# Attention and bilinear feed-forward on one core: the last tile's bias as two minima, low parts and q's split ordered behind the reciprocal, two subtractions of x ordered behind the gate product

## The chip, the cores and the metric

The kernel runs on one core of a Trainium2 chip. The metric is the device time of one execution in microseconds (us), the median over the runs shown. The kernel before took 1290.13 us (median of three runs, 1284.51 to 1292.95). The profile and the trace are those of one further execution. A core has five engines with a queue of instructions each: TensorE (PE in the profile, its weight loads are PEld), VectorE (DVE), ScalarE (ACT), GpSimd (POOL) and SyncE (SP), which here issues transfers. Each queue is worked off in order.

## The reference

Block-causal attention over 8 batches of 8 heads, 576 positions and 64 dimensions, then a bilinear feed-forward layer over all 4,608 tokens with 512 model and 1,536 inner dimensions, all in float32:

```python
def _attn_ref(q, k, v):
    B, H, S, D = q.shape                      # 8, 8, 576, 64
    block, scale = 64, 1.0 / np.sqrt(D)
    scores = scale * np.matmul(q, k.transpose(0, 1, 3, 2))
    pos = np.arange(S)
    mask = (pos[:, None] // block) >= (pos[None, :] // block)
    scores = np.where(mask, scores, -1000000000.0)
    scores = scores - np.max(scores, axis=-1, keepdims=True)
    attn = np.exp(scores)
    attn = attn / (np.sum(attn, axis=-1, keepdims=True) + 1e-09)
    return np.matmul(attn, v)

def reference(q, k, v, moe_w_a, moe_w_b, moe_w_out):
    o = _attn_ref(q, k, v)                    # 8, 8, 576, 64
    x = o.transpose(0, 2, 1, 3).reshape(4608, 512)
    return ((x @ moe_w_a) * (x @ moe_w_b)) @ moe_w_out
```

## The kernel before, in words

**Precision.** Most products are made from a high and a low part: a copy to the type fp32r on ACT (names with `h`: `ah`, `xh`, `hh`) and the rest, source minus copy, on DVE or POOL (names with `l`: `al`, `xl`). The first eight heads work in plain float32 (`NATIVE`).

**Attention, a head.** The queries of a head stand in tiles of 128 rows, t = 0 to 3, where tile t sees the keys up to its own end; the 64 rows at both ends of the sequence share one *side tile*. `softmax(i)` makes the scores of the side tile and of tile 3 on PE, then their negated maxima `nm` on DVE (line 400). These two tiles overlap: the rows in the lower half of the partitions have scores in both, so that both need the smaller of their two negated maxima, while in the upper half each tile keeps its own. The two columns of the bias `nb` (line 421) hold that. Exponentials run on ACT with `nm` or `nb` as bias and leave sums in `sm` (line 403). Tiles 0, 1 and 2 follow. Then DVE makes the row sums `rc` (lines 434 and 438) and their reciprocal (line 441), and POOL multiplies the exponentials `e` by it (line 444), tile by tile from 3 down.

`turn(i)` follows for t = 3 down to 0: PE transposes the scaled exponentials into `tp` (line 467), of which there are two buffers in PSUM, ACT copies it to `ah` (line 469), and DVE subtracts to give the low part `al` (line 471). A `tp` buffer is free for the tile after next when both have been done. `values(i)` multiplies v by `ah` (line 516) and by `al` (lines 520 and 522).

**Attention, the loop.** A slot handles one head: the table `SLOT` puts the maxima of head s, the transposes of heads s - 1 and s - 2 and the values of head s - 2 in turn. Heads go in pairs (even, odd), whose q and k are loaded together (lines 324 and 325, `kp` and `qp`), split into high and low (`split_q`, line 341; `split_k`, line 346) and spread by further transfers on SP (lines 360 and 361). In the even slot stand the split and the loads of a later pair.

**The first pass of the feed-forward layer** (`first_pass`, 4 of 12 tiles of the inner dimension) runs on PE in between: its products (line 217, `ps` from `xh` and `xl`, 128x288) fill PE between the steps of the heads. `convert_w` meanwhile turns the weights into the form that PE uses, from 512 KB loads `raww` (line 124). The last third of the kernel are two more passes (`ps_` = 0 and 1) over six pairs of token tiles of 384 tokens. `sums_x` loads and combines x (lines 664 to 688): differences on DVE (674 to 676 and 679, `xt`), high parts on ACT (677 to 681), low parts on DVE (684, 685) and, for the second half of the rows (`kp` = 1), on POOL (687, 688). `pair_unit` makes the products of one inner tile in PSUM banks `psy`, `psx`, `psw`, `psv` (line 705) and the gate product `u` on DVE (lines 723 to 733), from which ACT and POOL make the high and the low part of h (lines 110 and 113). `pair_out` multiplies by the output weights (line 751), adds the partial sum of the pass before on DVE (line 810) and stores it (line 811). Partial sums are loaded at line 806. The generator for the next tile's x is started in the fourth inner tile's turn and its remaining steps run ahead of `pair_out`. The *switch of passes* is the place, at about 1000 us in the trace, where pass 0's last tile ends and pass 1's first begins; the x of pass 1's first tile has the name `0_6`.

**What sets the order.** All this is written as one program; a scheduler then arranges the instructions of each engine by its own priorities. `behind_of(ins, key)` adds an order without a wait: `ins` shall stand behind the instruction that `last[key]` names. Keys are "nb" (the bias), "rc" (the row sums) and "hf" (the last gate product `u` of an inner tile). Before the change the sums stand behind "nb", as do the low parts of the tile that is transposed together with the side tile (`SIDE_T`) and of tile 0; the conversion of weights is paced by "hf".

## Time and profile before

| what | value |
|---|---|
| median of the runs (lowest, highest) | 1290.13 us (1284.51, 1292.95) |
| the profiled execution | 1293.99 us |
| its span in the trace | 1292.2 us |
| its mean granted clock of TensorE | 0.984 |
| instructions in the trace | 23401 |
| moved by transfers | 196.58 MB, mean 152 GB/s |

The span runs from the first to the last recorded instruction; the execution's own time has 1.8 us more around it. Stretches in the trace are counted from the span's start. Attention with the first pass fills it up to about 625 us, the end of the first pass and the turn to the second goes to 720, pass 0 to about 1000 and pass 1 to the end. Here is the granted clock in 40 equal slices of 32.3 us, in tenths (9 is 90% or more), beside the busy share of PE and VectorE:

```profile
PE   9998999999999999999998998999999899999998
DVE  6877778778878787887789999899976576577563
PEclk8999999999999999999998999999999899999999
```

And this is the chain that ended last, followed back from the last instruction, as shares of the span by engine and by line:

```profile
PE 61%; DVE 21%; issue 6%; DMA 5%; ACT 4%; POOL 2%; SPq 0%; ACTq 0%; DVEq 0%; POOLq 0%
PE pso_z L751 13%; PE ps L217 8%; PE psx_z L705 6%; PE psw_z L705 6%; PE psv_z L705 6%; PE tp L467 5%; DVE al L471 3%; PE s L394 3%; PE pso L217 3%; DVE nm L400 3%; PE psy_z L705 3%; PE av L522 2%; PE av L506 2%; POOL e L444 2%; DMA kp<-kT 1%
```

A row of a timeline reads: start in us, length, engine, line, operation, what it writes and reads with shapes, and in brackets how long the engine was idle before it and what ended that. A row of groups reads: line, engine, operation and operands, number, then busy time in us, mean in ns, idle time before.

### The profile page before, as it was taken

Reading aid. Unit: us, or ns where it says so; the run is one execution under the profiler, and the core shown is the slowest. Engines: PE = TensorE matmul, PEld = TensorE weight load, DVE = VectorE, ACT = ScalarE, POOL = GpSimd, SP = SyncE. Lnnn points to the kernel's source line nnn. Section 1 sums busy time; section 2 is a strip of 40 time slices with the busy share of each in tenths; the row PEclk is TensorE's granted clock in tenths of the full one; section 3 lists DMA queues with packets and bytes.
Section 4 is the critical chain, followed back from the end, with each engine's and each line's share of the span. In section 5 each row is a group of like instructions: output and inputs, shape, how many; then the busy total and the mean of one; then the engine's idle time right before and its main releaser. Section 6 shows DMA issues by size and latency. Waiting matters only on the chain.

```text
span 1292.2 us, 23401 instructions
## 1 busy us (share of the span) xinstructions
PE 1242.7 (96%) x7849; PEld 1177.4 (91%) x7849; DVE 1000.4 (77%) x2325; ACT 686.9 (53%) x1722; POOL 545.0 (42%) x681
## 2 busy tenths in 40 slices
PE   9998999999999999999998998999999899999998
PEld 5677989999999999999997998999999899999998
DVE  6877778778878787887789999899976576577563
ACT  5787777788787887887745423233322222222210
POOL 4667555555565555655522223223123123123231
PEclk8999999999999999999998999999999899999999
DMA  5466667766676666677224355464466442242131
GB/s 194 138 188 169 170 170 180 176 166 171 165 182 171 168 178 164 163 187 172 82 93 149 111 190 163 163 195 157 159 205 238 160 148 65 83 147 87 61 98 62
DMA packets 93496, 196.58 MB, mean 152 GB/s; under 512 B 11968, under 2 KB 52928, under 8 KB 93376
## 3 DMA queue, kind: packets, MB, share of 16 engines
q1 hardware_dynamic: 88768, 185.64, 50.8%
q10 hardware_dynamic: 4608, 9.44, 2.0%
q8 instruction: 63, 1.03, 0.3%
q14 instruction: 57, 0.47, 0.1%
HBM read 96.47 MB, written 47.19 MB: 111 GB/s over the span
## 4 chain that ended last, share of the span: by engine, by line
PE 61%; DVE 21%; issue 6%; DMA 5%; ACT 4%; POOL 2%; SPq 0%; ACTq 0%; DVEq 0%; POOLq 0%
PE pso_z L751 13%; PE ps L217 8%; PE psx_z L705 6%; PE psw_z L705 6%; PE psv_z L705 6%; PE tp L467 5%; DVE al L471 3%; PE s L394 3%; PE pso L217 3%; DVE nm L400 3%; PE psy_z L705 3%; PE av L522 2%; PE av L506 2%; POOL e L444 2%; DMA kp<-kT 1%
## 5 line engine op out<-in xcount | busy, mean ns | idle before, releaser
L113 POOL TENSOR_TENSOR h_z<-u_z,h_z 128x384 fp32r<-128x384 f32 x96 | 112.9, 1176 | 400.8 <-ACT h_z L110 378.2
L217 PE MATMUL ps<-xh,wab 128*128 128x288 f32 x1024 | 245.9, 306 | 0.0
L444 POOL TENSOR_SCALAR e<-e,rc 128x512 f32<-128x512 f32 (+3 forms) x256 | 152.3, 608 | 154.6 <-DVE rc L441 148.1
L751 PE MATMUL pso_z<-h_z,wo 128*128 128x384 f32 x1152 | 203.8, 335 | 3.5 <-POOL h_z L113 3.5
L751 PEld LDWEIGHTS pso_z<-h_z,wo 128*128 128x128 f32 x1152 | 199.6, 188 | 5.8 <-POOL h_z L113 5.8
L471 DVE TENSOR_TENSOR al<-tp,ah 128x512 fp32r<-128x512 f32 x224 | 138.8, 620 | 63.7 <-ACT ah L469 61.6
L217 PEld LDWEIGHTS ps<-xh,wab 128*128 128x128 f32 x1024 | 173.7, 190 | 3.6
L467 PE MATMUL tp<-ident,e 128*128 128x128 f32 x832 | 136.3, 279 | 18.5 <-POOL e L444 11.6
L217 PE MATMUL ps<-xl,wab 128*128 128x288 f32 x512 | 152.8, 299 | 0.2 <-POOL xl L113 0.2
L110 ACT CAST h_z<-u_z 128x384 fp32r<-128x384 f32 x96 | 49.4, 514 | 167.2 <-DVE u_z L730 162.1
L469 ACT CAST ah<-tp 128x512 fp32r<-128x512 f32 x224 | 119.2, 534 | 35.0 <-PE tp L467 33.3
L467 PEld LDWEIGHTS tp<-ident,e 128*128 128x128 f32 x832 | 99.3, 142 | 36.2 <-POOL e L444 21.4
L217 PE MATMUL pso<-hh,wo 128*128 128x288 f32 x512 | 128.5, 312 | 3.2 <-ACT hh L110 3.2
L705 PE MATMUL psx_z<-xh,wab 128*128 128x384 f32 x384 | 118.5, 344 | 9.0 <-DVE u_z L723 8.6
L403 ACT ACTIVATE e<-s,nm 128x192 f32<-128x192 f32 (+2 forms) x192 | 101.8, 531 | 36.7 <-DVE nm L400 30.1
L705 PE MATMUL psw_z<-xh,wab 128*128 128x384 f32 x384 | 117.3, 341 | 0.8 <-DVE u_z L725 0.8
L705 PE MATMUL psv_z<-xh,wab 128*128 128x384 f32 x384 | 117.2, 340 | 0.5 <-DVE u_z L727 0.4
L400 DVE TENSOR_REDUCE nm<-s 128x1 f32<-128x128 f32 (+3 forms) x256 | 110.2, 432 | 4.4
L217 PEld LDWEIGHTS ps<-xl,wab 128*128 128x128 f32 x512 | 97.3, 190 | 3.9 <-POOL xl L113 0.4
L217 PEld LDWEIGHTS pso<-hh,wo 128*128 128x128 f32 x512 | 89.2, 193 | 5.3 <-ACT hh L110 3.9
L113 POOL TENSOR_TENSOR v<-vr,v 128x320 fp32r<-128x320 f32 x56 | 49.4, 883 | 85.6 <-ACT v L110 63.7
L394 PE MATMUL s<-k,q 128*128 128x256 f32 x336 | 81.7, 325 | 2.6 <-ACT e L403 1.4
(143 smaller groups left out, 2913.3 us busy)
## 6 DMA issues: line engine op xcount, KB each, us to landing
k<-kp SPq DMA_DIRECT2D x112, 288.0 KB, 4.0
xr<-xd SPq DMA_DIRECT2D x48, 384.0 KB, 3.5
pt<-part SPq DMA_DIRECT2D x96, 192.0 KB, 3.5
q<-qp SPq DMA_DIRECT2D x112, 160.0 KB, 2.8
raww<-wab SPq DMA_DIRECT2D x24, 512.0 KB, 3.8
qp<-qT SPq DMA_DIRECT2D x32, 320.0 KB, 3.1
vr<-vm SPq DMA_DIRECT2D x64, 160.0 KB, 3.4
kp<-kT SPq DMA_DIRECT2D x32, 288.0 KB, 3.1
```

The source lines that it names most:

```text
L110: nc.scalar.copy(hi, src)
L113: return lo_eng.tensor_tensor(lo, src, f32(hi), op=ALU.subtract)
L217: mm = nc.tensor.matmul(ps, w_, d_, start=(i == 0), stop=(i == n - 1))
L394: mark = nc.tensor.matmul(ps[:, :w], qm[:, q0[t]:q0[t] + P], kk[:, :w], start=(i == 0), stop=(i == len(ks) - 1))
L400: nc.vector.tensor_reduce(nm[:, t:t + 1], view, axis=AX.X, op=ALU.max, negate=True)
L403: nc.scalar.activation(out, view, AF.Exp, bias=bias, accum_out=sm[:, t, :1])
L444: nc.gpsimd.tensor_scalar(ev, ev, rc[:, t:t + 1], 1.0, op0=ALU.mult, op1=ALU.mult)
L467: mark = nc.tensor.transpose(tp[:, c], src, ident)
L469: nc.scalar.copy(ah[:, :m, cols], tp[:, :m])
L471: return nc.vector.tensor_tensor(al[:, :m, cols], tp[:, :m], f32(ah[:, :m, cols]), op=ALU.subtract)
L705: nc.tensor.matmul(ps, wt[:, i, iw], j[:, ix], start=start and kp == 0 and i == 0 and j is xh, stop=kp == KP - 1 and i == 1, skip_group_ch ...
L751: nc.tensor.matmul(ps, wt[:, a, osl], b, start=i == 0, stop=i == 3 * len(fs) - 1)
```

## The change

It has three parts.

1. *The bias.* The old form is one instruction over two columns: column by column, the smaller of (the other tile's negated maximum plus a constant `apart`) and the tile's own; `apart` is a large number in the upper half, so that each keeps its own there, and zero in the lower half. The new form are two reductions on 64 partitions each: over a single column in the upper half, which copies it, and over both columns, read twice by a broadcast, in the lower half. `apart` and the two fills on POOL that make it go.
2. *The order behind the reciprocal.* The key "rc" now names the reciprocal, not the row sum ahead of it. Two low parts of the transposed exponentials (`SIDE_T` and tile 0) stand behind it, in place of behind the bias, and so does the low part of q's split, which had no order of this kind.
3. *The subtractions of x.* For the x of pass 1's first tile (`0_6`) the first two of four subtractions stand behind the last gate product.

```diff
-    apart = const.tile([P, 1], F32, name="apart")
-    nc.gpsimd.memset(apart[:BLK], -NEG)
-    nc.gpsimd.memset(apart[BLK:], 0.0)
...
-        nc.vector.scalar_tensor_tensor(qp[:, 0], qp[:, 0], SCALE, qp[:, 1], op0=ALU.mult, op1=ALU.subtract)
+        behind_of(nc.vector.scalar_tensor_tensor(
+            qp[:, 0], qp[:, 0], SCALE, qp[:, 1], op0=ALU.mult, op1=ALU.subtract), "rc")
...
-        last["nb"] = nc.vector.scalar_tensor_tensor(nb, nm[:, LAST:][:, ::-1], apart, nm[:, LAST:], op0=ALU.add, op1=ALU.min)
+        two = nm[:, LAST:]
+        nc.vector.tensor_reduce(nb[:BLK], two[:BLK, :, None], axis=AX.X, op=ALU.min)
+        last["nb"] = nc.vector.tensor_reduce(
+            nb[BLK:], two[BLK:, None, :].to_broadcast([P - BLK, 2, 2]), axis=AX.X, op=ALU.min)
...
-        last["rc"] = nc.vector.tensor_reduce(rc, sm, axis=AX.X, op=ALU.add)
+        ins = nc.vector.tensor_reduce(rc, sm, axis=AX.X, op=ALU.add)
         if not native:
-            behind_of(last["rc"], "nb")
+            behind_of(ins, "nb")
...
-        nc.vector.reciprocal(rc, rc)
+        last["rc"] = nc.vector.reciprocal(rc, rc)
...
             if t == SIDE_T and not native:
                 yield mark
-                behind_of(lower(), "nb")
+                behind_of(lower(), "rc")
                 continue
             if not native:
                 ins = lower()
                 if t == 0:
-                    behind_of(ins, "nb")
+                    behind_of(ins, "rc")
...
-        v.tensor_tensor(t[:, 1], b[:, 1], a[:, 1], op=ALU.subtract)
-        v.tensor_tensor(a[:, 1], a[:, 1], a[:, 0], op=ALU.subtract)
+        for ins in (v.tensor_tensor(t[:, 1], b[:, 1], a[:, 1], op=ALU.subtract),
+                    v.tensor_tensor(a[:, 1], a[:, 1], a[:, 0], op=ALU.subtract)):
+            if nm == f"0_{NT2}":
+                behind_of(ins, "hf")
```

Since a scheduler arranges the rest, the instructions move in further places than the diff names. The lines of the kernel after are two or three lower up to line 338 and beyond it, and one to three higher from line 434 on (400 becomes 398, 421 becomes 420 and 421, 441 becomes 442, 444 becomes 445, 471 becomes 472).

**An even head in the steady part.** On VectorE in the slot of head 2 of batch 5; `sl`, `s1`, `s0` are score tiles (3 with the side tile, 1, 0), `nm5_2` and `nb5_2` maxima and bias of that head, `rc5_1` the sum of the head before, `tp5_0` and `al5_0` the transposes and low parts of the head before that. Before:

```order
L400 TENSOR_REDUCE nm5_2_6164<-sl5_2_6167 128x1
L400 TENSOR_REDUCE nm5_2_6164<-s15_2_6168 128x1
L421 SCALAR_TENSOR_TENSOR nb5_2_6166<-nm5_2_6164,apart_107 128x2
L434 TENSOR_REDUCE rc5_1_6004<-sm1_127 128x5
L471 TENSOR_TENSOR al5_0_6086<-tp5_0_1_6148,ah5_0_6085 128x4x128
L438 TENSOR_REDUCE rc5_1_6004<-sm1_127 64x2
L471 TENSOR_TENSOR al5_0_6086<-tp5_0_0_6199,ah5_0_6085 128x2x128
L441 RECIPROCAL rc5_1_6004<-rc5_1_6004 128x5
L429 MEMSET s05_2_6211 64x64
L400 TENSOR_REDUCE nm5_2_6164<-s05_2_6211 128x1
```

After:

```order
L398 TENSOR_REDUCE nm5_2_6203<-sl5_2_6206 128x1
L472 TENSOR_TENSOR al5_0_6125<-tp5_0_2_6175,ah5_0_6124 128x4x128
L398 TENSOR_REDUCE nm5_2_6203<-s15_2_6207 128x1
L430 MEMSET s05_2_6251 64x64
L420 TENSOR_REDUCE nb5_2_6205<-nm5_2_6203 64x2
L421 TENSOR_REDUCE nb5_2_6205<-nm5_2_6203 64x2
L435 TENSOR_REDUCE rc5_1_6042<-sm1_124 128x5
L398 TENSOR_REDUCE nm5_2_6203<-s05_2_6251 128x1
L439 TENSOR_REDUCE rc5_1_6042<-sm1_124 64x2
L442 RECIPROCAL rc5_1_6042<-rc5_1_6042 128x5
L472 TENSOR_TENSOR al5_0_6125<-tp5_0_1_6187,ah5_0_6124 128x4x128
L472 TENSOR_TENSOR al5_0_6125<-tp5_0_0_6239,ah5_0_6124 128x2x128
```

The low parts of tiles 1 and 0 went behind the reciprocal; the maximum of tile 0 and the low part of tile 2 came ahead of it. TensorE in the same slot, `ps` being products of the first pass, `av` the head's values; before:

```order
L217 MATMUL ps0_4_0_0_6186<-xh4_0_0_5164,wab0_79 128x288
L467 MATMUL tp5_0_0_6199<-ident_102,e0_0_110 128x128 x2
L217 MATMUL ps0_4_0_0_6186<-xh4_1_0_5480,wab0_79 128x288
L217 MATMUL ps0_4_0_0_6186<-xl4_1_0_5481,wab0_79 128x288
L217 MATMUL ps0_4_0_0_6186<-xh4_1_0_5480,wab0_79 128x288
L217 MATMUL ps0_4_0_0_6186<-xh4_2_0_5796,wab0_79 128x288
L394 MATMUL s05_2_6211<-k25_2_5955,q25_2_5954 128x256 x2
L217 MATMUL ps0_4_0_0_6186<-xl4_2_0_5797,wab0_79 128x288
L217 MATMUL ps0_4_0_0_6186<-xh4_2_0_5796,wab0_79 128x288
L217 MATMUL ps0_4_0_0_6186<-xh4_3_0_6112,wab0_79 128x288
L217 MATMUL ps0_4_0_0_6186<-xl4_3_0_6113,wab0_79 128x288
L516 MATMUL av5_0_6222<-ah5_0_6085,v25_0_6039 128x512
```

After:

```order
L392 MATMUL s05_2_6251<-k25_2_5993,q25_2_5992 128x256 x2
L217 MATMUL ps0_4_0_0_6226<-xl4_2_0_5834,wab0_79 128x288
L217 MATMUL ps0_4_0_0_6226<-xh4_2_0_5833,wab0_79 128x288
L217 MATMUL ps0_4_0_0_6226<-xh4_3_0_6151,wab0_79 128x288
L468 MATMUL tp5_0_0_6239<-ident_102,e0_0_107 128x128 x2
L217 MATMUL ps0_4_0_0_6226<-xl4_3_0_6152,wab0_79 128x288
L217 MATMUL ps0_4_0_0_6226<-xh4_3_0_6151,wab0_79 128x288
L217 MATMUL ps1_4_0_0_6270<-xh4_0_0_5197,wab0_79 128x288
L217 MATMUL ps1_4_0_0_6270<-xl4_0_0_5198,wab0_79 128x288
L517 MATMUL av5_0_6262<-ah5_0_6124,v25_0_6078 128x512
```

The transposes of tile 0 (`tp5_0_0`) moved from ahead of tile 0's scores to behind them, four products ahead of the values `av`.

**The end of the start-up.** SP's queue where k and q of heads 6 and 7 of batch 1 are loaded (`kp1_6`, `qp1_6`); `raww` is a weight load. Before:

```order
L361 DMA k21_5_1372<-kp1_4_936 64x1152
L325 DMA qp1_6_1161<-qT 128x640
L333 DMA vr1_5_1616<-vm 128x320
L124 DMA raww4_1_9800<-wab 128x1024
L324 DMA kp1_6_1162<-kT 128x576
L333 DMA vr1_6_1768<-vm 128x320
```

After:

```order
L359 DMA k21_5_1381<-kp1_4_941 64x1152
L322 DMA qp1_6_1168<-qT 128x640
L330 DMA vr1_5_1626<-vm 128x320
L330 DMA vr1_6_1779<-vm 128x320
L321 DMA kp1_6_1169<-kT 128x576
L124 DMA raww4_1_9861<-wab 128x1024
```

The load of k now stands ahead of the weight load, and the v of head 6 ahead of both.

**The switch of passes.** POOL around the last inner tile of pass 0 (`h0_z0_5_7` and `h1_z0_5_7` are the high and low parts of h of inner tile 7, 6 being the one before, `xl_0_6_1` the low part of the next pass's x). Before:

```order
L113 TENSOR_TENSOR h1_z0_5_6_0_13136<-u0_z0_5_6_13139,h0_z0_5_6_0_13135 128x384
L113 TENSOR_TENSOR h1_z0_5_7_1_13216<-u1_z0_5_7_13218,h0_z0_5_7_1_13215 128x384
L687 TENSOR_TENSOR xl_0_6_1_13268<-xr3_0_13022,xh_0_6_1_13258 128x768
L688 TENSOR_TENSOR xl_0_6_1_13268<-xt_0_6_1_13259,xh_0_6_1_13258 128x384
L113 TENSOR_TENSOR h1_z0_5_7_0_13214<-u0_z0_5_7_13217,h0_z0_5_7_0_13213 128x384
```

After:

```order
L113 TENSOR_TENSOR h1_z0_5_6_0_13197<-u0_z0_5_6_13200,h0_z0_5_6_0_13196 128x384
L690 TENSOR_TENSOR xl_0_6_1_13329<-xr3_0_13083,xh_0_6_1_13319 128x768
L113 TENSOR_TENSOR h1_z0_5_7_1_13277<-u1_z0_5_7_13279,h0_z0_5_7_1_13276 128x384
L113 TENSOR_TENSOR h1_z0_5_7_0_13275<-u0_z0_5_7_13278,h0_z0_5_7_0_13274 128x384
L691 TENSOR_TENSOR xl_0_6_1_13329<-xt_0_6_1_13320,xh_0_6_1_13319 128x384
```

The first part of x's low part stands ahead of both h parts now, the second behind both. SP in the same place, where `xr` are the loads of x for the next tile, `part1` stores of partial sums and `pt0` loads of them. Before:

```order
L664 DMA xr0_1_13470<-xd_57 128x768
L811 DMA part1_59<-pt1_0_5_0_13092 128x384
L811 DMA part1_59<-pt1_1_5_0_13094 128x384
L811 DMA part1_59<-pt1_2_5_0_13096 128x384
L664 DMA xr1_1_13472<-xd_57 128x768
L806 DMA pt0_2_5_0_13298<-part0_58 128x384
L806 DMA pt0_3_5_0_13305<-part0_58 128x384
L811 DMA part1_59<-pt1_3_5_0_13098 128x384
L811 DMA part1_59<-pt0_0_5_0_13100 128x384
L664 DMA xr2_1_13474<-xd_57 128x768
```

After:

```order
L814 DMA part1_59<-pt1_0_5_0_13153 128x384
L814 DMA part1_59<-pt1_1_5_0_13155 128x384
L665 DMA xr0_1_13531<-xd_57 128x768
L809 DMA pt0_2_5_0_13359<-part0_58 128x384
L809 DMA pt0_3_5_0_13366<-part0_58 128x384
L665 DMA xr1_1_13533<-xd_57 128x768
L814 DMA part1_59<-pt1_2_5_0_13157 128x384
L814 DMA part1_59<-pt1_3_5_0_13159 128x384
L814 DMA part1_59<-pt0_0_5_0_13161 128x384
L665 DMA xr2_1_13535<-xd_57 128x768
```

The first load of x goes out behind two stores, the second behind the two loads of partial sums.

## The prediction

> **What bounds the kernel now.** I read the page's first part, then the busy times by stage, then what TensorE (PE) waits for in each stage, then single stretches. First the page, then the stages: stretch, its length, then busy microseconds of PE, of its weight loads (PEld), VectorE (DVE), ScalarE (ACT) and GpSimd (POOL), granted clock, DMA share and GB/s.
>
> ```profile
> PE 1242.7 (96%) x7849; PEld 1177.4 (91%) x7849; DVE 1000.4 (77%) x2325; ACT 686.9 (53%) x1722; POOL 545.0 (42%) x681
> ```
>
> ```profile
> 100.00:200.00 100.00, 91.66 (x619) 85.13 (x618) 75.90 (x230) 74.55 (x210) 59.69 (x84) 0.97 0.66 174
> 200.00:625.00 425.00, 415.05 (x3004) 398.77 (x3003) 336.23 (x1008) 338.90 (x945) 244.03 (x366) 1.00 0.67 168
> 720.00:990.00 270.00, 260.71 (x1454) 251.95 (x1453) 240.08 (x408) 88.23 (x153) 74.99 (x58) 1.00 0.51 171
> 990.00:1030.00 40.00, 35.77 (x191) 35.44 (x191) 23.42 (x37) 6.21 (x11) 9.31 (x7) 0.91 0.56 196
> ```
>
> PE is busy for 1242.7 of 1292.2 us, so what can be won is its idle time, some 50 us, and the time at a granted clock below 1. In the steady attention (200 to 625) that is 10 us at full clock; around the switch of passes (990 to 1030) it is 4.2 us in 40, with the clock at 0.91. What PE itself waits for, first in 200 to 625, then in 0 to 200 (total, times, longest):
>
> ```profile
> PE tp L467 <- POOL e L444: 8.2, 20, 0.7
> ```
>
> ```profile
> PE tp L467 <- POOL e L444: 3.4, 7, 1.1
> ```
>
> So the steady part's only large wait is one of 0.41 us on average, twenty times in 425 us: once in two heads. Here is such a place: DVE, then POOL, then PE (start, length, and in brackets the idle time before it and what ended it).
>
> ```profile
> 402.72 0.85 DVE L421 SCALAR_TENSOR_TENSOR nb<-nm,apart 128x2 f32<-128x2 f32 x1
> ...
> 403.57 0.67 DVE L471 TENSOR_TENSOR al<-tp,ah 128x512 fp32r<-128x512 f32 x1
> ...
> 404.46 0.42 DVE L471 TENSOR_TENSOR al<-tp,ah 128x256 fp32r<-128x256 f32 x1
> 404.80 0.18 DVE L441 RECIPROCAL rc<-rc 128x5 f32<-128x5 f32 x1
> ...
> 405.20 0.36 DVE L400 TENSOR_REDUCE nm<-s 128x1 f32<-128x192 f32 x1
> ```
>
> ```profile
> 405.08 1.31 POOL L444 TENSOR_SCALAR e<-e,rc 128x512 f32<-128x512 f32 x2 [1.52 <-DVE rc L441]
> ```
>
> ```profile
> 405.83 0.66 PE L467 MATMUL tp<-ident,e 128*128 128x128 f32 x4 [0.38 <-POOL e L444]
> ```
>
> The chain is bias (0.85), sum, two low parts (0.67 and 0.42), reciprocal, scaling on POOL, transposes. POOL has idled 1.52 us for the reciprocal and PE 0.38 for POOL.
>
> **The change, part by part.**
>
> *Bias as two minima.* The row of the old instruction by line (busy, mean ns), then minimum/median/maximum ns of it and of a reduction of the same 64x2 shape:
>
> ```profile
> L421 DVE SCALAR_TENSOR_TENSOR nb<-nm,apart 128x2 f32<-128x2 f32 x64 | 26.2, 410 | 1.7
> ```
>
> ```profile
> L421 DVE SCALAR_TENSOR_TENSOR nb<-nm,apart x64: 151/224/871, 8.8 to 630.6; 128x2 f32<-128x2 f32 x64
> ```
>
> ```profile
> L438 DVE TENSOR_REDUCE rc<-sm x64: 156/157/159, 15.1 to 639.1; 64x2 f32<-64x6 f32 x64
> ```
>
> Two reductions at 157 ns are 0.31 us, against 0.22 at the median and 0.85 at the place above, where POOL was in a two-input subtraction. Over 64 heads that is 26.2 - 64 x 0.314 = 6.1 us less DVE work; DVE has 89 us of slack in the steady part, so by itself it is worth 0, and it counts only inside the chain above. The Trainium skill (VectorE: DVE Perf Modes, Rules for kernel authors) speaks against this part: it calls the reduction the slowest DVE operation and advises restructuring it. By that rule the bias gets dearer, by 0.09 us a head against the median, 5.8 us of DVE work in all; the rows of this case, with a mean of 410 ns for the old form and a spread of 3 ns for the reduction, say the opposite where it matters. The two fills of the removed constant are over before its first use at 8.8 us: 0.
>
> *Low parts behind the reciprocal.* At the place above the two low parts leave the chain (0.67 + 0.42 = 1.09 us), the bias gets shorter by 0.85 - 0.31 = 0.54, and two things come in by the order: the low part of tile 2 ahead of the side tile's maximum, 0.67, and the maximum of tile 0, 0.36. Net 1.09 + 0.54 - 0.67 - 0.36 = 0.60 us earlier. That exceeds the mean wait of 0.41, so I drop all 8.2 us. Of the 3.4 us in 0 to 200 I count half, 1.7, since other work of POOL stands ahead of the scaling in the start-up. Together -9.9.
>
> What is late next: the order now puts tile 0's transposes nine matmuls later in every second head, four matmuls ahead of the product that needs their copy. The copy's latency, from the neighbouring head (PE, with one matmul left out, then ACT), and one place where it was waited for:
>
> ```profile
> 412.12 0.38 PE L467 MATMUL tp<-ident,e 128*128 128x128 f32 x2
> ...
> 412.47 0.29 PE L217 MATMUL ps<-xl,wab 128*128 128x288 f32 x1
> 412.61 0.43 PE L217 MATMUL ps<-xh,wab 128*128 128x288 f32 x2
> ```
>
> ```profile
> 412.54 0.37 ACT L469 CAST ah<-tp 128x256 fp32r<-128x256 f32 x1 [0.73 <-PE tp L467]
> ```
>
> ```profile
> 110.53 0.97 PE L516 MATMUL av<-ah,v 128*128 128x512 f32 x4 [0.46 <-ACT ah L469]
> ```
>
> From the first transpose to the end of the copy are 0.79 us; two transposes and a matmul take 0.35 (412.12 to 412.47) and a matmul 0.14, so the two transposes and four matmuls cover 0.35 + 3 x 0.14 = 0.77. So next to nothing is missing if ACT is free, and up to 0.46 if it is not. I take 0.15 in each of 27 such heads, nearer to the free case since ACT idled 0.73 us there (27 is every second of the heads that have low parts, rounded down): +4.0. Net of this part -5.9.
>
> The low parts themselves can end later by their own time at most, 1.09 us; the products that read them start well after:
>
> ```profile
> 407.02 0.91 PE L522 MATMUL av<-al,v 128*128 128x256 f32 x4
> ```
>
> Here they ended at 404.46 + 0.42 = 404.88, 2.1 us before, so 0. Without that cover each tenth of lateness costs 2.7 us.
>
> *q's split.* It moves from the odd head to behind the even head's reciprocal, some 7 us. SP's next issue of the same pair:
>
> ```profile
> 429.20 0.46 SPq L360 DMA_DIRECT2D q<-qp  x1
> ```
>
> The even head that now holds the split has its reciprocal some 20 us after that of the place above, near 425, so the low half goes out near 426, and the queue stands until 429.20 anyway: 0. If it passed 429.2, k's halves and the next load of k would shift one to one.
>
> At the end of the start-up the new order does show: the load of one pair's k (batch 1, heads 6 and 7) now goes out ahead of a 512 KB weight load.
>
> ```profile
> 118.10 0.38 SPq L124 DMA_DIRECT2D raww<-wab  x1
> 118.58 0.37 SPq L324 DMA_DIRECT2D kp<-kT  x1
> ```
>
> ```profile
> 126.29 0.67 ACT L346 CAST kp<-kp 128x576 fp32r<-128x576 f32 x1 [3.48 <-DMA kp<-kT]
> ```
>
> ```profile
> 128.82 0.96 PE L467 MATMUL tp<-ident,e 128*128 128x128 f32 x7 [3.15 <-DVE al L471]
> ```
>
> ```profile
> kp<-kT SPq DMA_DIRECT2D x32, 288.0 KB, 3.1
> ```
>
> ```profile
> 125.00:150.00 25.00, 20.98 (x142) 19.73 (x141) 16.77 (x51) 18.82 (x53) 14.54 (x21) 0.93 0.55 141
> ```
>
> This load took over 7 us to land where the median is 3.1; ACT stood still 3.48 us, and PE 3.15. At 3.1 us it would land near 122, before ACT asks for it. The gain lies between 0 and 3.15 + 1.75 (a clock of 0.93 over 25 us) = 4.9; I take two thirds, 3.2, since the queue's order is certain and its times are not.
>
> *Subtractions held back.* Those for the next pass's first tile leave the output stage of the tile before; half of them go into the last unit of the pass, where DVE waits for PE between its additions, and half between the output additions behind it. The wait at the switch is this chain (SP's two last loads of x, DVE, PE):
>
> ```profile
> 997.89 0.41 SPq L664 DMA_DIRECT2D xr<-xd  x1
> ...
> 1004.00 0.43 SPq L664 DMA_DIRECT2D xr<-xd  x1
> ```
>
> ```profile
> 1008.95 0.56 DVE L674 TENSOR_TENSOR xt<-xr,xr 128x384 f32<-128x384 f32 x1 [3.35 <-DMA xr<-xd]
> ```
>
> ```profile
> 1011.81 0.69 PE L705 MATMUL psx_z<-xh,wab 128*128 128x384 f32 x1 [4.23 <-DVE u_z L723]
> ```
>
> DVE waits for x, its additions wait behind it, SP's stores wait for the additions, and the next x load stands behind the stores. By the new order the second load goes out behind two stores in place of three, but also behind two partial-sum loads: about 0.5 us earlier. The addition that frees the last load comes one instruction sooner: 0.5. So the chain ends 1.0 us earlier. Against it, POOL now takes an x part before the last h part:
>
> ```profile
> 988.19 1.46 POOL L113 TENSOR_TENSOR h_z<-u_z,h_z 128x384 fp32r<-128x384 f32 x1 [5.85 <-ACT h_z L110]
> 989.61 2.59 POOL L687 TENSOR_TENSOR xl<-xr,xh 128x768 fp32r<-128x768 f32 x1
> ```
>
> ```profile
> 986.07 0.84 ACT L677 CAST xh<-xr 128x768 fp32r<-128x768 f32 x1 [4.88 <-PE psv_z L705]
> ```
>
> ```profile
> 989.71 13.31 PEld L751 LDWEIGHTS pso_z<-h_z,wo 128*128 128x128 f32 x77 [0.17 <-POOL h_z L113]
> ```
>
> The x part's input is a copy like that of 986.07, ready at 986.91. With 2.59 us first, the h part ends at 986.9 + 2.59 + 1.46 = 990.96, where PE took it at 989.71: some 1.2 us of standing. That falls inside the later wait, which then is 4.23 - 1.0 - 1.2, near 2 us long. The clock of 0.91 over 40 us is 3.6 us lost; with half the wait I take 1.4 of it back. This part: -2.4, between +1.2 and -4.6.
>
> **The sum.** -5.9 - 3.2 - 2.4 = -11.5 us. The profiled execution took 1293.99 us (span 1292.2), so 1282.5; it stands 3.9 us above the median of 1290.13, and against that median I forecast 1278.6.
>
> **The rivals.** *Waits change places*: in the even heads the copy is late by the 0.46 of the row at 110, not by 0.15. Then 27 x 0.46 = 12 us eat the 9.9, and about half of the other parts remains: 1290.1 + 2.5 - 2.8 = 1290. For it: ACT is 80% busy in the steady part (338.9 of 425). Against it: ACT's idle 0.73 just there.
>
> *Slower*: tile 2's copy and low part now follow the exponential of tile 2 on ACT, and tile 0's transposes write into tile 2's buffer. The transposes move back too, by nine matmuls (9 x 0.14 = 1.26 us), about as far, which speaks against it. No row shows the margin; I bound the lateness by one low part and one copy, 0.67 + 0.37 = 1.04 us. Beyond 0.37 us (9.9 over 27 heads) the gain is gone; at the bound, and with half of the other parts, 1290.1 + 28.1 - 9.9 - 2.8 = 1305.5; a loss of 1% begins at 0.95.
>
> *Both slow-clock stretches vanish*: PE waits of some 2 us leave no slow clock, as the 9.3 us of waits between 720 and 990 left the clock at 1.00. Then the switch gives 1.0 + 3.6 and the start-up all 4.9: -5.9 - 4.9 - 4.6 = -15.4, or 1274.7. Against it, a wait of 1.42 us stands in a stretch at 0.93, so I give the case less than a fifth:
>
> ```profile
> 182.52 0.50 PE L394 MATMUL s<-k,q 128*128 128x256 f32 x2 [1.42 <-ACT e L403]
> ```
>
> ```profile
> 175.00:200.00 25.00, 23.20 (x157) 22.14 (x155) 16.61 (x51) 18.28 (x52) 13.82 (x22) 0.93 0.66 168
> ```
>
> This is what the Trainium skill (TensorE: Matmul & The Clock Gate, Part 1) would have: the clock halves only after an idle window of about 3.4 us. The stretch around 182 does not agree with that: no idle window there was longer than the 1.42 us.
>
> *The change doesn't reach the path*: POOL's scaling is held by something else than the reciprocal. The row at 405.08 names the reciprocal, so this has no share of its own.
>
> **How the numbers follow.** Forecast 50%, waits change places 25%, clock stretches vanish 17%, slower 8%. The range reaches from below the third rival (1272, with some 3 us of scatter between runs) to just past the first (1291); its own range for the forecast is 1273 to 1284. I count 1% (12.9 us) as about what a measurement of this kernel tells from no change. Below 1277.2 lie most of the third rival and a third of the forecast: 0.15 + 0.17 = 0.32. Above 1303 lies the slower one, counted whole: 0.08. The rest is 0.60.
>
> **What would show it.** Right: PE's wait for POOL's e in 200 to 625 falls below 1 us; the bias rows are near 157 ns without spread; POOL's idle time ended by rc shrinks; no 3 us wait near 129; the switch's wait is near 2 us. Wrong: a wait of PE for ah or for al once in two heads; SP's q halves past 429; more than 2 us on h at the switch.

## The result

| | median | lowest to highest | runs |
|---|---|---|---|
| before | 1290.24 us | 1284.51 to 1292.95 | 6 |
| after | 1279.07 us | 1276.53 to 1281.83 | 6 |

The ratio is 0.9918 (95% interval 0.9893 to 0.9943), so the change takes 0.8% off, 11 us. The forecast was 1278.6 us, in a range of 1272 to 1291. Among the runs of the experiments below, one of q's split alone and one of the kernel before took over 3000 us; the ratios leave them out. The profiled execution of the kernel after took 1281.83 us with a span of 1279.8, at a mean granted clock of 0.988.

### The profile page after: what moved, and what is told of

Same layout as the page of the kernel before. It is cut to its first block, busy times and chain, and to the rows that moved or that the text cites. A ratio compares the mean times of both kernels' runs of the same rounds, so it can differ in the third digit from the quotient of the medians.

```text
span 1279.8 us, 23524 instructions
## 1 busy us (share of the span) xinstructions
PE 1239.3 (97%) x7849; PEld 1173.2 (92%) x7849; DVE 999.2 (78%) x2389; ACT 683.6 (53%) x1722; POOL 554.9 (43%) x679
## 4 chain that ended last, share of the span: by engine, by line
PE 71%; DVE 15%; DMA 4%; issue 4%; ACT 3%; POOL 2%; SPq 1%; ACTq 0%; DVEq 0%; POOLq 0%
PE pso_z L754 13%; PE ps L217 12%; PE tp L468 7%; PE psx_z L708 6%; PE psw_z L708 6%; PE psv_z L708 6%; PE pso L217 4%; PE s L392 4%; PE psy_z L708 3%; PE av L517 3%; PE av L523 3%; PE sl L392 2%; DMA kp<-kT 2%; PE av L507 2%; DVE sw L147 1%
## 5 line engine op out<-in xcount | busy, mean ns | idle before, releaser
L217 PE MATMUL ps<-xh,wab 128*128 128x288 f32 x1024 | 241.8, 304 | 1.2 <-ACT a L241 1.2
L472 DVE TENSOR_TENSOR al<-tp,ah 128x512 fp32r<-128x512 f32 x224 | 131.6, 608 | 31.5 <-ACT ah L470 31.0
L470 ACT CAST ah<-tp 128x512 fp32r<-128x512 f32 x224 | 116.4, 531 | 50.3 <-PE tp L468 47.5
L398 DVE TENSOR_REDUCE nm<-s 128x1 f32<-128x192 f32 (+3 forms) x256 | 109.9, 431 | 2.4
```

The source lines that it names most:

```text
L217: mm = nc.tensor.matmul(ps, w_, d_, start=(i == 0), stop=(i == n - 1))
L398: nc.vector.tensor_reduce(nm[:, t:t + 1], view, axis=AX.X, op=ALU.max, negate=True)
L470: nc.scalar.copy(ah[:, :m, cols], tp[:, :m])
L472: return nc.vector.tensor_tensor(al[:, :m, cols], tp[:, :m], f32(ah[:, :m, cols]), op=ALU.subtract)
```

## The profile after

The first part of the page, then the stages as in the prediction (length, busy time of PE, PEld, DVE, ACT and POOL, granted clock, DMA share, GB/s).

```profile
PE 1239.3 (97%) x7849; PEld 1173.2 (92%) x7849; DVE 999.2 (78%) x2389; ACT 683.6 (53%) x1722; POOL 554.9 (43%) x679
```

```profile
100.00:200.00 100.00, 95.16 (x669) 88.72 (x668) 84.99 (x260) 80.71 (x226) 63.14 (x87) 1.00 0.71 188
200.00:625.00 425.00, 421.78 (x3031) 404.81 (x3030) 333.28 (x1058) 337.85 (x950) 256.95 (x370) 1.00 0.67 166
720.00:990.00 270.00, 259.29 (x1449) 250.41 (x1448) 237.54 (x396) 84.96 (x146) 77.51 (x58) 1.00 0.53 175
990.00:1030.00 40.00, 37.91 (x207) 37.59 (x206) 22.52 (x42) 10.65 (x19) 7.20 (x7) 0.96 0.41 142
```

PE's busy time is 3.4 us less for the same work. Its idle time fell from 49.5 to 40.5 us: in the steady attention from 10 to 3.2 us of 425, in 100 to 200 from 8.3 to 4.8, with the clock there from 0.97 to 1.00. The stretches are the same in time, not in work, so to see where the time went I took the moments at which the same work is reached in both traces: the exponential of each head's side tile, and the first copy of each product unit of the two later passes.

```
reached in the trace        before     after   after - before
head 12                     120.65    122.03     +1.4
head 16                     163.54    159.97     -3.6
head 20                     205.87    198.75     -7.1
head 22                     225.66    220.89     -4.8
head 62                     621.26    610.74    -10.5
unit 22 (end of pass 0)     972.87    961.94    -10.9
unit 24 (first of pass 1)  1005.55    995.94     -9.6
unit 26                    1026.18   1013.62    -12.6
unit 46                    1258.32   1245.95    -12.4
```

These are two single executions, so part of the differences is scatter. Two of the experiments below show how much: the kernel with the subtractions alone has the order of the kernel before on VectorE, ScalarE, GpSimd and SP up to about 946 us, and the kernel with eleven matmuls has that of the kernel after.

```
us in the trace       before   subtractions   after   eleven
                               alone                  matmuls
start to head 12      120.65   116.43         122.03  119.92
heads 12 to 16         42.89    42.89          37.94   37.82
heads 16 to 20         42.32    39.94          38.78   38.94
heads 20 to 22         19.79    19.79          22.14   22.65
heads 22 to 62        395.60   396.04         389.85  388.83
```

Ahead of head 12 the same order scatters by 4 us, so the +1.4 there says nothing. There are three gains, at the places that the prediction names: 5 us between heads 12 and 16, another 1 to 3.5 us up to head 20 (the trace before has a half-clock stretch of 3.4 us there, from 184 us on, and the second trace of its order has none); 5.7 to 7.2 us over the forty heads from 22 to 62; and 1.6 us around the switch. And there is a loss that it doesn't name, in both traces: 2.3 to 2.9 us between heads 20 and 22.

**The steady part.** What PE waits for in 200 to 625 (total, times, longest):

```profile
PE tp L468 <- POOL e L445: 1.4, 1, 1.4
PE tp L468 <- DVE al L472: 1.4, 4, 0.4
```

The twenty waits for the scaled exponentials (8.2 us) are one. On the weight loads the same waits are longer; before:

```profile
PEld tp L467 <- POOL e L444: 13.0, 21, 0.9
```

After, that row has 1.7 us, in one wait, and two others are new:

```profile
PEld tp L468 <- POOL xl L113: 3.3, 8, 0.6
PEld av L517 <- ACT ah L470: 3.3, 20, 0.2
```

The second of them was looked at closely: twenty times, once in two heads, the product av stands 0.165 us for the copy ah of tile 0. Each is too short to be a row among PE's own waits. An even head of the kernel after, DVE then POOL, at 396 us:

```profile
396.69 0.14 DVE L420 TENSOR_REDUCE nb<-nm 64x2 f32<-64x2 f32 x1
396.85 0.15 DVE L421 TENSOR_REDUCE nb<-nm 64x2 f32<-64x4 f32 x1
...
397.68 0.19 DVE L442 RECIPROCAL rc<-rc 128x5 f32<-128x5 f32 x1
397.79 0.98 DVE L472 TENSOR_TENSOR al<-tp,ah 128x512 fp32r<-128x512 f32 x2
...
398.97 0.98 DVE L338 SCALAR_TENSOR_TENSOR qp<-qp 128x640 f32<-128x640 f32 x1
```

```profile
397.97 1.31 POOL L445 TENSOR_SCALAR e<-e,rc 128x512 f32<-128x512 f32 x2 [1.00 <-DVE rc L442]
399.26 0.94 POOL L445 TENSOR_SCALAR e_s<-e_s,rc 128x128 f32<-128x128 f32 x1
```

The order is the one of the diff: bias, sums, reciprocal, and only then the two low parts and q's split. At this place POOL's idle time for the reciprocal is 1.00 us, where the place in the prediction had 1.52.

**The start-up.** SP's queue and ACT at the load of k for heads 6 and 7 of batch 1, then the busy times of the stretch:

```profile
119.50 0.37 SPq L321 DMA_DIRECT2D kp<-kT  x1
119.91 0.43 SPq L124 DMA_DIRECT2D raww<-wab  x1
```

```profile
123.43 0.68 ACT L344 CAST kp<-kp 128x576 fp32r<-128x576 f32 x1
```

```profile
125.00:150.00 25.00, 24.46 (x175) 23.06 (x175) 21.90 (x66) 20.11 (x56) 15.91 (x23) 1.00 0.65 159
```

The load goes out ahead of the weight load, ACT works on k 3.9 us after its issue and without idle time before it (7.7 us and 3.48 us of idle before the change), and the stretch ran at full clock.

**The loss at 200 us.** PE, then what POOL did ahead of the exponentials that PE waited for:

```profile
201.63 1.11 PE L468 MATMUL tp<-ident,e 128*128 128x128 f32 x4 [1.42 <-POOL e L445]
```

```profile
198.92 1.42 POOL L345 TENSOR_TENSOR kp<-kp 128x576 f32<-128x576 f32 x1 [3.18 <-ACT kp L344]
200.30 1.88 POOL L445 TENSOR_SCALAR e<-e,rc 128x512 f32<-128x512 f32 x2
```

The split of k came late to POOL and stood ahead of the scaling, though the reciprocal was done at 198.44. The wait of 1.42 us was followed by 3.4 us at half clock.

**The switch.** PE at the last products of pass 0 and at the wait itself, and POOL ahead of the first:

```profile
980.08 5.15 PE L754 MATMUL pso_z<-h_z,wo 128*128 128x384 f32 x28 [1.05 <-POOL h_z L113]
...
1000.06 0.67 PE L708 MATMUL psx_z<-xh,wab 128*128 128x384 f32 x1 [2.09 <-DVE u_z L726]
```

```profile
976.22 2.13 POOL L690 TENSOR_TENSOR xl<-xr,xh 128x768 fp32r<-128x768 f32 x1 [4.81 <-ACT xh L683]
978.30 1.72 POOL L113 TENSOR_TENSOR h_z<-u_z,h_z 128x384 fp32r<-128x384 f32 x1
```

The wait is 2.09 us in place of 4.23, and h stands 1.05 us behind the low part of x.

## The experiments

Times are medians; each was timed in five rounds beside the kernel before, whose medians in the three groups of runs were 1289.76, 1289.74 and 1289.02 us.

### One part alone

**The bias alone** (the first part of the diff).

> The kernel before with the bias as two minima and nothing else. Theory (each of the two steady parts shortens the chain to the reciprocal by more than the wait): the reciprocal of the even heads comes some 0.5 us earlier (0.85 - 0.31), TensorE's waits for the scaled exponentials in 200 to 625 fall from 8.2 us to under 2, the 3 us wait near 129 us and the 4.2 us wait at the switch stay; time 1290 - 7 = 1283 us. Rival (the reduction is the dearer form, by 0.09 us a head against the old median): the waits stay at 8 us or more and the time is 1290 us or above.

Measured: 1286.31 us, ratio 0.9972 (0.9957 to 0.9988). PE's wait in 200 to 625:

```profile
PE tp L467 <- POOL e L444: 2.6, 10, 0.4
```

By the medians 3.5 us off, half of what was expected. The waits fell by 5.6 us where over 6 were worked out, and the reciprocal gained half of the 0.5 us. From the first product of the scores `sl` to the end of the reciprocal the median over the even heads from 20 to 60 fell from 3.99 to 3.75 us, and over the odd heads it rose from 3.28 to 3.48. So the new form is the shorter one where the old one was slow, and the longer one elsewhere. The rival's price is real in the odd heads: there the exponential that waits for the bias begins at 2.05 us in place of 1.96, later by 0.09 as worked out. PE doesn't wait in those heads.

**The low parts alone** (the keys of `SIDE_T` and tile 0, and the reciprocal as "rc").

> The kernel before with only the two low parts of the transposes behind the reciprocal. Theory: the reciprocal of the even heads comes 1.0 us earlier (two low parts out, one fill in), the waits for the scaled exponentials in 200 to 625 fall from 8.2 us to under 2, no new wait for copies or low parts appears; start-up and switch as before; time 1283 us. Rival (the low parts come late instead): TensorE's waits for al or ah rise by 4 us or more and the time stays at 1288 to 1292 us.

Measured: 1274.7 us, ratio 0.989 (0.9865 to 0.9915): by the medians 15 us off, where 7 were expected, and 4 us less than the whole change takes. PE's wait in 200 to 625:

```profile
PE tp L467 <- POOL e L444: 0.3, 1, 0.3
```

No wait for al or ah replaced it; the reciprocal came 0.64 us earlier in the even heads (3.35, where 1.0 was expected) and 0.74 in the odd (2.54). The expectation counted PE's own waits, 8.2 us. The weight loads' waits for the exponentials fell from 13.0 to 0.9 us, and from head 22 to 62 the trace took 11.0 us less. Another 3.3 went between heads 12 and 16, which was not expected: the wait near 129 us is still there (2.84 us), but no half-clock stretch follows it. That may be chance, since in the later run without q's split one follows a wait of 2.1 us at the same place.

**q's split alone.**

> The kernel before with only the low part of q's split behind the reciprocal. This is what moves the load of k (batch 1, heads 6 and 7) ahead of the weight load, and it also puts the low part of tile 2 ahead of the bias in the even heads. Theory: start-up 3 to 5 us shorter, without the 3 us wait near 129 us; in the even heads the reciprocal comes some 0.7 us later, so that the waits for the scaled exponentials in 200 to 625 rise from 8.2 to about 21 us; time 1290 - 4 + 13 = 1299 us. Rival (the split's place is harmless to the chain): waits stay at 8 us, time 1286 us.

Measured: 1283.44 us, ratio 0.9947 (0.9924 to 0.9969). The price in the steady part was wrong. The reciprocal of the even heads came when it came before (4.01 against 3.99 us), and PE waited less:

```profile
PE tp L468 <- POOL e L445: 2.3, 2, 1.2
```

The order on TensorE had moved too: in all even heads from 20 to 60, 29 matmuls stand between the scores `sl` and the transposes that wait for the exponentials, where there were 27, so that the same reciprocal is early enough. In the kernel after there are 27 again. What the order costs is the wait for ah: the same row as after (3.3 us, 20 times, 0.2 the longest) stands among its weight loads, and in no kernel without this order. The start-up gained as expected: the wait near 129 us is gone, and heads 12 to 16 took 38.7 us against 42.9.

**The subtractions alone.**

> The kernel before with only the first two subtractions of the next pass's x held behind the gate product. Theory: everything up to 960 us as before, the wait of 4.2 us at the switch becomes one of about 2 us, time 1.5 to 2.4 us less: 1288 us. Rival (the low part of x on GpSimd now delays h by 1.2 us and gives it back): the switch is no shorter, time 1290 us or more.

Measured: 1288.31 us, ratio 0.9982 (0.9966 to 0.9998). The wait at the switch is as after:

```profile
PE psx_z L707 <- DVE u_z L725: 2.0, 1, 2.0
```

The parts alone add up to 3.5 + 15.1 + 6.3 + 1.5 = 26 us, the whole change gives 11. Bias, low parts and q's split all shorten the same waits, and one part may take back what another gives. The second group looks for which.

### One part less, and the load's order by itself

**The change without q's split.**

> The kernel after with q's split left where it was (bias, low parts and subtractions as in the kernel after). Theory: it is the order of q's split that moves tile 0's transposes back on TensorE and puts tile 2's low part ahead of the bias; without it the products av no longer wait for the copies ah (over heads 24 to 60 their starts fall back by 3 us to the intervals of the kernel before), the switch keeps its shorter wait, and the load of k is behind the weight load again, with the 3 us wait near 129 us. Time: 1274.7 (the low parts alone) - 1.5 = 1273 us. Rival (the loss against the low parts alone comes from the bias or the held subtractions): the time stays near 1279 us.

Measured: 1274.34 us, ratio 0.9886 (0.9855 to 0.9916). For heads 24 to 60 I summed the distances from each matmul's start to the one before it, by what the matmul writes; this counts waits too short for a row. All kernels have the same matmuls.

```
us, heads 24 to 60            before   low parts  q's split  after  without   without
                                       alone      alone             q's split  the bias
all                           356.8    346.8      354.4      351.9  344.4      353.0
transposes tp (504)            71.3     60.6       65.1       62.7   58.7       63.2
values av 128x448 (72)         13.9     14.5       15.4       15.4   14.0       15.5
values av 128x512 (72)         12.0     12.1       13.8       13.7   12.0       13.7
products ps 128x288 (864)     118.9    119.0      119.4      119.2  119.0      119.3
```

The three kernels with q's split behind the reciprocal have some 3.3 us more in the two values rows, the others less than 1. That is the wait for ah, and without the split's order it is gone, as expected. So is the weight loads' wait for xl. By the two further traces of unchanged orders (357.3 and 350.9 us), "all" scatters by 1 us or less. The wait for k's low parts near 129 us is back as expected, with 2.1 us. The switch was not as expected:

```profile
983.53 1.34 SPq L664 DMA_DIRECT2D xr<-xd  x1
```

```profile
PE psx_z L707 <- DVE u_z L725: 3.5, 1, 3.5
```

SP's issue of the last load of x took 1.34 us where it took 0.38 after and with the subtractions alone, so that the held subtractions brought nearly nothing here. The order of the queue is the same. What makes this issue longer stays open; the low parts alone show it too (1.36 us).

**The weight load behind the load of k, alone.**

```diff
-        nc.sync.dma_start(raw.rearrange("p n w -> p (n w)"), src)
+        ins = nc.sync.dma_start(raw.rearrange("p n w -> p (n w)"), src)
+        if nm == "w4_1":
+            behind_of(ins, "kp")
...
-        nc.sync.dma_start(kp[:, 1], kT[b, h:h + 2].rearrange("h d s -> (h d) s"))
+        ins = nc.sync.dma_start(kp[:, 1], kT[b, h:h + 2].rearrange("h d s -> (h d) s"))
+        if p == 7:
+            last["kp"] = ins
```

> The kernel before with one order added: the 512 KB weight load (inner tile 4, second piece) goes out behind the load of k for heads 6 and 7 of batch 1. Theory: this order is what q's split brought to the start-up; the load of k lands in some 3 us instead of over 7, the 3.15 us wait near 129 us and the slow clock behind it go, steady part and switch as before; time 1289.8 - 3.2 = 1286.6 us, at most 4.9 less. Rival (something else ends last there, since a wait of 2.8 us by the same chain stands in the run with the low parts alone and its start-up was shorter all the same): no change, 1290 us.

Measured: 1286.59 us, ratio 0.9969 (0.995 to 0.9987). ACT's cast of k and PE's next wait:

```profile
123.77 0.67 ACT L350 CAST kp<-kp 128x576 fp32r<-128x576 f32 x1 [0.98 <-DMA kp<-kT]
```

```profile
126.31 0.95 PE L471 MATMUL tp<-ident,e 128*128 128x128 f32 x7 [0.69 <-DVE al L475]
```

By the medians two transfers in the other order are worth 3 us, and 3.15 us of PE's wait became 0.69.

**Low parts, subtractions and the load's order together.**

> The kernel before with the low parts behind the reciprocal, the subtractions held back, and the weight load behind the load of k; the bias and q's split as before. Theory: the three gains lie in different stretches and add up: 1274.7 - 1.5 - 3 = 1270 us, no wait over 2.5 us anywhere between 50 and 600 us. Rival (the load of k only uncovers the next late thing of the start-up): 1273 us.

Measured: 1271.96 us, ratio 0.9866 (0.984 to 0.9893). No wait of PE between 50 and 600 us is over 1.3 us, as expected. The switch's wait is 3.2 us, again with a long issue of the load (1.29 us), which may be what is missing to 1270; the gain of the low parts between heads 12 and 16 may be another part, since the load's order gains in the same stretch.

**The change without the bias.**

> The kernel after with the old bias (low parts, q's split and subtractions as in the kernel after). Theory: with the low parts out of the chain the bias alone decides little, the reciprocal of the even heads comes 0.4 us later than in the kernel after, and one or two of TensorE's waits in two hundred microseconds come back: 1280 us, within 2 us of the kernel after. Rival (the bias carries the gain of the steady part): waits for the scaled exponentials back at 5 us or more, 1285 us.

Measured: 1278.92 us, ratio 0.9912 (0.9883 to 0.9942): the same as the whole change. The reciprocal of the even heads did not come later but 0.13 us earlier (3.36 against 3.49), so this step of the theory was wrong. With the low parts out of the chain, the two minima decide nothing that can be measured.

### The bias again, and the wait at the switch filled

**Bias, low parts, subtractions and the load's order.**

> The kernel after with q's split left where it was and, instead, the weight load put behind the load of k by an order of its own. Theory: the bias still gives something beside the low parts, since heads 24 to 60 took 344.4 us with both against 346.8 and 347.6 us in the two runs with the low parts and the old bias; with the load's order the time is 1270 us (1272 - 2). Rival (with the low parts out of the chain the bias gives nothing): 1272 us, as without it.

Measured: 1271.96 us, ratio 0.9872 (0.9854 to 0.9889): the rival's figure. In its trace heads 24 to 60 took 345.4 us against 347.6 without the bias, so a microsecond or two may be there, but no measurement of the whole shows it. Against the kernel after, this one has the order between two transfers in place of q's split: 7 us less, and the intervals of the two ratios (0.9854 to 0.9889 and 0.9893 to 0.9943) don't overlap.

**Eleven matmuls in the wait at the switch of the kernel after.**

```diff
         v.tensor_tensor(u, x, u, op=ALU.add)
+        if nm == f"z1_0_{F1 + F2}":
+            for _ in range(11):
+                nc.tensor.matmul(y, w[:, 0][:, 0, 0], xs[0][0][:, 0], start=True, stop=True)
         yield from prod(x, X2, False)
```

> The kernel after with eleven matmuls of 128x384 put into TensorE's wait at the switch of passes; what they write is read by nobody. Theory (the slow clock answers to idle time of TensorE of about 2 us within one stretch of 3.4 us): they take 11 x 0.16 = 1.8 us of the 2.1 us wait, no stretch at half clock follows the switch, the granted clock over 990 to 1030 us is 1.00 in place of 0.96, and the time falls by 1.7 us to 1277.4 us. Rival (the slow clock there follows from something else): the clock stays at 0.96 and the time at 1279 us or a little above.

Measured: 1278.7 us, ratio 0.9918 (0.9898 to 0.9938). The same stretch of the kernel after, then of this one (the last three columns are granted clock, DMA share and GB/s):

```profile
990.00:1000.00 10.00, 7.97 (x46) 7.64 (x44) 6.24 (x12) 3.30 (x5) 0.00 (x0) 1.00 0.95 320
1000.00:1003.40 3.40, 3.34 (x10) 3.34 (x11) 1.12 (x3) 0.00 (x0) 0.00 (x0) 0.52 1.03 407
```

```profile
990.00:1000.00 10.00, 9.69 (x56) 9.37 (x55) 6.91 (x14) 3.30 (x5) 0.00 (x0) 1.00 0.91 320
1000.00:1003.40 3.40, 3.40 (x21) 3.40 (x20) 2.21 (x5) 0.51 (x1) 0.01 (x1) 1.00 1.04 399
```

The mechanism is as expected: no idle time, no slow clock, and 21 matmuls in those 3.4 us where there were 10. In the trace the switch (units 24 to 26) took 16.1 us against 17.7. In the time of the whole, 1.6 us are less than what can be measured.

**Seventeen such matmuls in the kernel with bias, low parts, subtractions and the load's order.**

> The kernel of the first run of this group with seventeen such matmuls in the wait at the switch, which was 3.2 to 3.5 us in the runs with the low parts and the held subtractions. Theory: both slow stretches behind the switch (6.8 us at half clock) go, 3.4 us less than without them: 1267 us. Rival: no change against 1270 us, or above it if the added matmuls last longer than the wait.

Measured: 1271.05 us, ratio 0.9859 (0.9839 to 0.9879). PE waits no more for x at the switch; but in this execution SP's issue of the last load took 0.38 us, so less than 3.2 us may have been there to fill. It is the fastest kernel of the study, by 8 us against the kernel after, whose interval begins (0.9893) above the end of this one's; against the kernel without the seventeen the difference of 0.9 us is not resolved.

## Why the prediction was right or wrong

The sum came out, in part by luck. The places were right; which part of the change acts at which place was not. By parts the forecast was -5.9 us for bias and low parts, -3.2 for q's split and -2.4 for the subtractions; the runs show by their medians some -15 for the low parts alone, +5 for q's split beside the other parts and -1.5 for the subtractions. Two errors of 8 to 9 us cancelled.

| term | forecast | found |
|---|---|---|
| waits for scaled exponentials, 0 to 625 | -9.9 | -7.6 (11.6 to 4.0 by the rows of waits) |
| waits for ah | +4.0 | +3.3 |
| load of k | -3.2 | -3.2 alone; -4.9 between heads 12 and 16 of the two traces, with what the low parts gain there |
| switch | -2.4 | -1.5 alone; -1.6 in the two traces |
| sum | -11.5 | -11.2 (medians) |

The found terms need not add up to the sum: the loss at 200 us, the weight loads' longer waits and those for xl stand in none of them.

- **The chain to the reciprocal.** Right: it came 0.50 us earlier in the even heads (3.99 to 3.49) where 0.60 was worked out, and nineteen of twenty waits went. Who did it was put together wrongly. I let bias and low parts add up (0.54 and 1.09); alone the low parts remove the waits (0.3 us left) and without the bias the time is the same. The bias and the low parts together were put at -9.9; the low parts alone took 15 us off. The term was too small since it counted PE's own waits, 8.2 us, and not the weight loads', 13.0.
- **The rule against the reduction.** The pair of reductions took 143 and 154 ns at the median, 0.30 us, against the 0.314 assumed. The Trainium skill (VectorE: DVE Perf Modes, Rules for kernel authors) calls the reduction the slowest operation of the engine. On these 64x2 tiles the trace agrees by 0.09 us in the odd heads and not in the even ones; in the odd heads PE doesn't wait.
- **The wait for ah.** Right in place and size: 0.15 us in every second head was forecast, 0.165 measured. The forecast tied it to the low parts. It belongs to q's split: with the low parts alone, or with the change without q's split, it isn't there.
- **q's split: 0.** This step failed. I looked only at SP's queue, where it indeed cost nothing, and took the new order of tile 2's low part and of tile 0's transposes for a result of the low parts. The single part shows that the split's order moves them. Leaving it out, the kernel took 1274.34 us in place of 1279.07, so by the medians the split costs some 5 us; the intervals of the two ratios overlap (0.9855 to 0.9916 and 0.9893 to 0.9943). With the load's order in place of the split it is 1271.96 us, and there they don't overlap. In the traces heads 24 to 60 show where: 344.4 us against 351.9, of it 3.2 in the two values rows, which is the wait for ah, and 4.0 ahead of transposes. For the latter the weight loads name POOL's xl (3.3 us from 200 to 625, with q's split only); why they wait for it stays open. It also brought the one gain that I credited to it, the load of k, and 3 us of that come as well from an order between two transfers.
- **The subtractions.** Right: a wait of near 2 us was forecast and 2.09 found, with 1.05 us of standing on h where 1.2 was worked out. The slow clock went from 6.8 to 3.4 us. As a saving it was 0.9 us less than forecast.
- **The rivals.** Waits did not change places to the full (3.3 us, not 12). The slower case did not come: from 200 to 625 PE's waits for al are 1.4 us in all. The clock stretches did not both vanish: the one near 130 did, the one at the switch was halved, and a new one came at 201 us.

What is not settled: why SP's issue of the last load of x took 1.1 to 1.4 us in some executions and 0.4 in others, and whether the bias gives a microsecond on top of the low parts. The issue is not a matter of the order: the kernels with bias, low parts, subtractions and the load's order, without and with the seventeen matmuls, have the same order on SP, VectorE, ScalarE and GpSimd, and it took 1.09 us in the one trace and 0.38 in the other.

## What to carry to other kernels

Work that nobody waits for soon, behind the instruction that everybody waits for: here two low parts alone gave by the medians 15 us, the whole change 11. An order added for one instruction is an order for all that the scheduler then moves, so cost it on each engine's new order and try each part alone; here a part that looked free took back 5 us or more. And a term that is worked out from two traces needs a second trace of one order, to see what scatters. When a wait is shorter than what a list of waits shows, look at the weight loads, or sum the distances between starts by kind.

## What the hardware showed

**The clock goes by idle time within fixed stretches.** The slow stretches last one or several times 3.413 us and lie on a grid of that length. Over the thirteen profiled executions I took every such stretch at full clock from 40 us to the last matmul, TensorE's idle time in it, and whether the next was at half clock:

```
TensorE idle in the stretch   stretches   next at half clock
under 1.0 us                  4482        0
1.0 to 1.5 us                 58          14
1.5 to 1.9 us                 30          20
1.9 us and more               34          34
```

So a wait of 2 us cost 1.7 us more when it fell into one stretch; by the table the same wait halved by an edge may cost nothing more. The eleven matmuls above show it from the other side. The Trainium skill (TensorE: Matmul & The Clock Gate, Part 1) gives the window of 3413 ns that runs by itself, which agrees, and an idle window of that length as the condition for the half clock, which does not: 1.9 us were always enough. The cases are not independent, since the executions share their places: the switch alone is eleven of the 34, and the fourteen between 1.0 and 1.5 us all lie between 40 and 79 us, thirteen of them at one place of each execution.

**VectorE and GpSimd in each other's way.** The scaling of the side tile on POOL, the same 128x128 work in every head, by minimum, median and maximum ns and by the mean in the kernel after:

```profile
L445 POOL TENSOR_SCALAR e_s<-e_s,rc x64: 364/373/943, 19.1 to 630.1; 128x128 f32<-128x128 f32 x64
```

```profile
L445 POOL TENSOR_SCALAR e_s<-e_s,rc 128x128 f32<-128x128 f32 x64 | 39.4, 616 | 0.0
```

It took 0.94 us at 399.26, while DVE had q's split from 398.97 to 399.95, which reads two operands from SBUF. From head 8 on the 24 scalings that fell beside q's split took 933 to 943 ns, the 32 others 364 to 381; in the kernel without q's split the mean is 426 ns. The Trainium skill (SBUF — State Buffer, SBUF: two separate sides) describes the port pair that the two engines share, as a lock held for a whole instruction by a VectorE operation with two SBUF inputs; the trace agrees, with 0.57 us more for the later one.

The old bias instruction, which reads two columns of `nm` and `apart`, shows the other side. At the place of the prediction (402.72, 0.85 us) POOL had two subtractions:

```profile
401.98 1.57 POOL L113 TENSOR_TENSOR xl<-xf,xh 128x288 fp32r<-128x288 f32 x2
```

In heads 20 to 60 of the kernel before, all 21 even heads had such a subtraction beside the bias: it took 261 to 871 ns and ended 16 to 23 ns after one of POOL's had ended. In the 20 odd heads POOL did nothing there, and it took 221 to 224 ns. Of the two minima, with one input each, 37 in the same heads of the kernel after fell beside work of POOL, and these took 141 to 155 ns.
